# Attention steps that begin with transposes in 64-row halves and end with the values of the same unit, in a kernel of attention and two layers of experts

## The chip, the cores and the metric

The kernel runs on one core of a Trainium2 chip. The metric is the time of one execution on the device in microseconds (us). TensorE (PE) multiplies, VectorE (DVE), ScalarE (ACT) and GpSimd (POOL) work on elements, SyncE (SP) issues most DMAs. Each engine takes its own instructions in the order in which the program wrote them; between engines only semaphores hold.

## The reference, cut to what matters

```python
def _attn_ref(q, k, v):                       # (2, 8, 576, 64) each
    scores = scale * np.matmul(q, k.transpose(0, 1, 3, 2))
    mask = (rel >= 0) & (rel < 128)
    scores = np.where(mask, scores + bias[None], -1000000000.0)
    scores = scores - np.max(scores, axis=-1, keepdims=True)
    attn = np.exp(scores)
    attn = attn / (np.sum(attn, axis=-1, keepdims=True) + 1e-09)
    return np.matmul(attn, v)
...
x = attn_out.transpose(0, 2, 1, 3).reshape(1152, 512)
for e in range(4):                            # first layer
    h = np.maximum(x @ w1[e], 0.0)
    out += p[:, e:e + 1] * (h @ w2[e])
...
h = x @ w_in                                  # second layer
return (h * np.cos(h)) @ w_out
```

A query attends to itself and to 127 keys before it. All is computed in float32.

## The kernel before, in words

**Attention** (to about 78 us). Queries come in nine units of 128 rows: units 1 to 4 and 5 to 8 are rows 64 to 575 of the two batches, unit 0 holds the first 64 rows of both and comes fifth. A step is one unit and one half `g` of the eight heads; steps 0 to 17 go through `attention`. For its step `k`, `att_scores` multiplies queries by the two key blocks of the window (four matmuls on 64-row tiles into two of three banks `ps_s`; 256, 192 or, for unit 0, 64 columns), VectorE adds the bias and takes the row's minimum (four reductions, L459), and ScalarE takes four exponentials (L465) into `p`. `att_sums` adds up the denominators of a whole unit on VectorE (`rec`, L477 and L480) and GpSimd spreads them (`wide`, L482). Two steps later `att_transpose` turns `p` on TensorE (L513) and two copies, one on VectorE (L522) and one on ScalarE (L524), bring it to `pt`; `att_factors` turns `wide` (L490, copy `rs` L494). Three steps later `att_pv` multiplies by the values (L550, L539 for unit 0) and, with the second half of the heads, VectorE multiplies by the factors (L560): 128 rows of `x` are done.

**Between the groups** stands `fill(k, s)`, three places in each step. It prepares weights on GpSimd (`jobs`), from step 12 on starts matmuls of the experts (`fills`: products of the first pair of weight columns `opening`, `leftover` and `turn_rows` for the 128 rows of unit 0, and the second layer's first tile `tile_begun`, `layer2(0, 0)`), and takes up to five pieces of the transformations (`move`).

**Transformations.** The first layer multiplies 1024 of the rows by a seven-product scheme (Strassen's). Each of four column tiles of 128 needs seven operands, each in two rounded parts: `hi` is rounded on ScalarE (L342), `lo` is the rest, subtracted on VectorE or GpSimd (L177). Operands of the first batch alone come from `own` (`B11`, `B21`), the other five from `transform`: four subtractions on VectorE, five `hi`, three `lo` on VectorE and two on GpSimd. They are generators in the list `moved`, oldest first, advanced piece by piece.

**Behind the attention** `steps(0)` (L974 on) runs two pairs of weight columns against the operands (`product`, L693), sums on VectorE (L757), `finish` rounds into `hpair` (ScalarE L682, VectorE L683); then come `left` (L723), the second layer (L843), and the other eleven groups in the same way, to 648.8 us.

Of the kernel before, what the change touches and what calls it, by code (L numbers as in the profile page):

```python
# [51 lines left out]
def tile_kernel(ctx, tc, qT, kT, v, probs, w1, w2, w_in, w_out, out):  # L52
# [24 lines left out]
    ptp = ap("ptp", bufs=4)  # L77
# [271 lines left out]
    def own(t, x1):  # L349

        hi, lo = parts(t)
        if t < NP and mm is None:
            yield
            yield
        hi(B11, x1[:, 0:2])
        yield
        lo(B11, x1[:, 0:2], nc.vector)
        hi(B21, x1[:, 2:4])
        yield
        lo(B21, x1[:, 2:4], nc.gpsimd)  # L360

    def transform(t, x1, x2, ps=None):

        hi, lo = parts(t)
        t1, t2 = (txp.tile([128, 2, 128], F32, name="tx", tag="tx") for _ in range(2))
        b11, b21, b12, b22 = x1[:, 0:2], x1[:, 2:4], x2[:, 0:2], x2[:, 2:4]
        if ps is None:
            yield
            yield
            ps = x2  # L370
        else:
            nc.scalar.activation(out=x2, in_=ps, func=AF.Copy)
        sub(nc.vector, t1, ps[:, 0:2], b11)
        sub(nc.vector, t2, ps[:, 2:4], t1)
        sub(nc.vector, b12, ps[:, 2:4], b12)
        yield

        hi(T2, t2)
        yield
        lo(T2, t2, nc.gpsimd)  # L380
        hi(T1, t1)
        yield
        lo(T1, t1, nc.vector)
        hi(T3, b12)
        yield
        lo(T3, b12, nc.gpsimd)
        sub(nc.vector, b21, b21, t2)
        hi(B22, b22)
        yield
        lo(B22, b22, nc.vector)  # L390
        hi(T4, b21)
        yield
        lo(T4, b21, nc.vector)

    def transformed(*args):
        if args[0] < NP - 1 or len(args) > 3:
            move(24)
        tr = transform(*args)
        if len(args) > 3:
            next(tr)  # L400
# [11 lines left out]

    def move_together(step):

        gens = moved[::-1]
        moved.clear()
        for _ in range(3):
            next(gens[0])
        next(step, None)
        while gens:  # L420
            gens = [g for g in gens if not next(g, True)]
# [81 lines left out]
    def att_transpose(u, g, pool=ps_t, tag="t_ps"):  # L503
# [3 lines left out]
        pT = []  # L507
        for m in range(2):
            tp = pool.tile([128, 2, 2, 128], F32, name="t_ps", tag=tag)
            pt = ptp.tile([128, 2, 2, 128], F32, name="pt", tag="pt")  # L510
            for bi, (j, o, ln) in enumerate(blocks):
                for hh in range(2):
                    nc.tensor.transpose(  # L513
                        tp[:ln, bi, hh, :], p[:, 2 * m + hh, o : o + ln], ident
                    )
            if len(set(lens)) == 1:
                sl = [(slice(0, lens[0]), slice(0, len(blocks)))]
            else:
                sl = [(slice(0, lens[k]), slice(k, k + 1)) for k in range(2)]
            for a, bb in sl:  # L520
                if m == 0:
                    nc.vector.tensor_copy(pt[a, bb], tp[a, bb])  # L522
                else:
                    nc.scalar.activation(out=pt[a, bb], in_=tp[a, bb], func=AF.Copy)  # L524
            pT.append(pt)
        state[u, g] = pT

    def att_pv(u, g):
# [4 lines left out]
        for m in range(2):  # L533
            if u == 0:
                for b in range(B):
                    for hh in range(2):
# [5 lines left out]
                            pT[m][:64, 0, hh, c], start=True, stop=True,  # L542
# [4 lines left out]
            for bi, (j, o, ln) in enumerate(blocks):  # L547
                for hh in range(2):
# [4 lines left out]
                        pT[m][:ln, bi, hh, :],  # L553
                        start=(bi == 0), stop=(bi == len(blocks) - 1),
                    )
        if g == 1:
# [9 lines left out]
            else:  # L566
                t = (u - 1) % NP
                x1 = xk[:, :, t * 128 : (t + 1) * 128]
                if u <= NP:
                    normal(x1)  # L570
                    moved.append(own(t, x1))
                else:
                    normal(x2s[t % 2])
                    transformed(t, x1, x2s[t % 2])
# [11 lines left out]
    def attention(fill):  # L586
        n = len(steps)
        at = lambda k, what, *more: what(*steps[k], *more) if 0 <= k < n else None
        for k in range(n):
# [4 lines left out]
            if k < 4:  # L594
                at(k - LAG, att_transpose)
            at(k, att_scores)
            at(k - 1, att_sums)
            fill(k, 0)
            if k >= 4:
                at(k - LAG, att_transpose)  # L600
            at(k - LAG, att_factors)
            fill(k, 1)
            at(k - LAG - 1, att_pv)
            fill(k, 2)

        at(n - 1, att_sums)
        at(n - 2, att_transpose)
        fill(n, 0)
        at(n - 1, att_transpose, ps_s, "s_ps")
        at(n - 3, att_pv)  # L610
        at(n - 1, att_factors)
        fill(n, 1)
        at(n - 2, att_pv)
        fill(n, 2)
        at(n - 1, att_pv)
        fill(n + 1, 0)
# [302 lines left out]
    with tc.manual_schedule():  # L919
# [24 lines left out]
        def tile_begun():  # L944
# [5 lines left out]
            (12, 1): lambda: opening(0, 3), (13, 1): lambda: early[0],  # L950
            (14, 1): lambda: leftover(False), (15, 1): lambda: leftover(True),
            (16, 1): lambda: turn_rows(0), (17, 1): lambda: opening(1, 1),
            (18, 1): tile_begun, (19, 0): lambda: layer2(0, 0),
        }

        def fill(k, s):
            if s == 0 and k < 1:
# [4 lines left out]
            if (k, s) == (2, 0):  # L962
                for _ in range(RAWS):
                    loads_ahead()
            if (k, s) == (4, 0):
                nc.sync.dma_start(out=pr, in_=probs.rearrange("(t p) e -> p t e", p=128))
                first_bias()
            if (k, s) == (9, 0):
                routing()
            if s == 0 and 4 <= k < 18:  # L970
                for _ in range(2 if k in (13, 15) else 1):
                    next(jobs)
            step = fills.get((k, s), lambda: None)()
            if step:  # L974
                next(step)
            if (k, s) == (19, 0):
                move_together(step)
                next(early[1])
            elif (k, s) != (17, 2):
                move((0, 3, 2)[s])  # L980
            if step:
                next(step, None)

# [158 lines left out]
```

## Time and profile before

| | us |
|---|---|
| median of 3 runs | 652.18 (650.93 to 652.92) |
| profiled execution | 650.58, span 648.8 |
| TensorE busy | 637.5 (98%) |
| VectorE busy | 448.1 (69%) |
| GpSimd busy | 347.7 (54%) |
| ScalarE busy | 325.4 (50%) |
| chain that ended last | TensorE 80%, ScalarE 9%, VectorE 6% |

The granted clock of TensorE is at its upper level, 2.4 GHz, in all 40 slices. Shares are means over stages: in attention ScalarE and VectorE are far busier than over the span. A row of the timeline holds one group of equal instructions: its start, the time to the end of the last one, and in brackets what ended an idle time before it. Ends of matmuls are modelled and overlap the next group, so lengths are better read from start to start or from the chain of waits.

### The profile page before, as it was taken

To read this page: it belongs to the slowest core of one execution; us is meant where nothing else is said; L and a number is where in the kernel's file an instruction comes from. 1 tells how busy PE (TensorE), PEld (TensorE's weight loads), DVE (VectorE), ACT (ScalarE), POOL (GpSimd) and SP (SyncE) were. 2 spreads that over 40 slices of the span, in tenths; PEclk is the share of its full clock that TensorE was granted. 3 is DMA by queue.
4 is the path that set the end of the run, shared out by engine and by line. 5 is a ranking of instruction groups with operands and counts; after the bars stand their busy time and mean duration, and the time that the engine had idled before them with its cause. 6 is when DMAs were issued, how large, how long until landed. Compare 5 with 4: busy or idle time off the path is not lost.

```text
span 648.8 us, 9141 instructions
## 1 busy us (share of the span) xinstructions
PE 637.5 (98%) x3320; PEld 522.6 (81%) x3320; DVE 448.1 (69%) x778; ACT 325.4 (50%) x688; POOL 347.7 (54%) x330
## 2 busy tenths in 40 slices
PE   8999999999999999999999999999999999999988
PEld 6777778888888888888888888888778878878866
DVE  6786879879879869779689532656864654654662
ACT  6897634444454353443353421355873663763750
POOL 1677529364265175274364470583479279378340
PEclk9999999999999999999999999999999999999999
DMA  9442204425426327337153120130102202201003
GB/s 253 139 130 100 75 25 155 154 82 194 147 71 228 123 73 243 106 115 223 36 167 126 33 99 0 33 97 2 33 1 66 66 1 66 65 1 65 18 12 119
DMA packets 39421, 60.64 MB, mean 93 GB/s; under 512 B 4688, under 2 KB 21840, under 8 KB 39376
## 3 DMA queue, kind: packets, MB, share of 16 engines
q1 hardware_dynamic: 38288, 59.67, 29.0%
q8 instruction: 26, 0.43, 0.3%
q10 hardware_dynamic: 1088, 0.39, 0.2%
q14 instruction: 19, 0.16, 0.1%
HBM read 49.30 MB, written 10.75 MB: 93 GB/s over the span
## 4 chain that ended last, share of the span: by engine, by line
PE 80%; ACT 9%; DVE 6%; issue 2%; POOL 1%; DMA 1%; POOLq 0%; ACTq 0%
PE o_ps L843 41%; PE o_ps L693 29%; PE o_ps L723 4%; ACT u L646 1%; ACT p L465 1%; ACT r L647 1%; ACT u L654 1%; PE x_ps L550 1%; PE s_ps L448 1%; ACT hpair L666 1%; DVE c L757 1%; PE t_ps L513 1%; DVE p L459 1%; DMA k<-kT 1%; PE l_ps L749 1%
## 5 line engine op out<-in xcount | busy, mean ns | idle before, releaser
L843 PE MATMUL o_ps<-w2t,hpair 128*128 128x512 f32 x1140 | 269.6, 392 | 2.8 <-POOL hpair L177 2.5
L843 PEld LDWEIGHTS o_ps<-w2t,hpair 128*128 128x128 f32 x1140 | 211.0, 188 | 47.7 <-POOL hpair L177 4.7
L693 PE MATMUL o_ps<-xs,w1t 128*128 128x512 f32 x720 | 169.5, 390 | 0.4 <-DVE h L177 0.2
L693 PEld LDWEIGHTS o_ps<-xs,w1t 128*128 128x128 f32 x720 | 134.6, 188 | 29.0 <-ACT xs L342 0.5
L177 POOL TENSOR_TENSOR w1t<-raw,w1t 128x512 fp32r<-128x512 f32 x48 | 64.4, 1355 | 87.5 <-ACT w1t L200 87.1
L177 POOL TENSOR_TENSOR w2t<-raw,w2t 128x512 fp32r<-128x512 f32 x48 | 64.4, 1362 | 64.1 <-ACT w2t L200 63.8
L177 POOL TENSOR_TENSOR w1t<-sm,w1t 128x512 fp32r<-128x512 f32 x48 | 64.2, 1349 | 36.7 <-ACT w1t L200 33.3
L693 PE MATMUL o_ps<-xz,w1t 128*128 128x512 f32 x288 | 70.9, 392 | 1.7 <-DVE c L757 1.7
L177 POOL TENSOR_TENSOR hpair<-u,hpair 128x512 fp32r<-128x512 f32 x32 | 41.6, 1312 | 45.9 <-ACT hpair L666 45.9
L693 PEld LDWEIGHTS o_ps<-xz,w1t 128*128 128x128 f32 x288 | 53.5, 188 | 14.9 <-DVE c L757 2.5
L864 DVE SCALAR_TENSOR_TENSOR accpair<-o_ps,pr,accpair 128x512 f32<-128x512 f32 x56 | 41.2, 745 | 28.0 <-PE o_ps L843 28.0
L299 ACT ACTIVATE cr<-cr 128x512 f32<-128x512 f32 x32 | 21.7, 679 | 77.0 <-DVE cv L293 77.0
L683 DVE SCALAR_TENSOR_TENSOR hpair<-o_ps,hpair 128x512 fp32r<-128x512 f32 x47 | 32.4, 689 | 21.5 <-ACT hpair L682 21.5
L682 ACT ACTIVATE hpair<-o_ps 128x512 fp32r<-128x512 f32 x47 | 28.2, 599 | 36.0 <-DVE o_ps L757 36.0
L200 ACT ACTIVATE w1t<-sm 128x512 fp32r<-128x512 f32 x44 | 27.4, 624 | 29.8 <-POOL sm L177 29.8
L650 DVE SCALAR_TENSOR_TENSOR u<-r,u 128x512 f32<-128x512 f32 x36 | 30.7, 853 | 14.3 <-ACT r L647 14.3
L465 ACT ACTIVATE p<-p,nmax 128x256 f32<-128x256 f32 (+2 forms) x72 | 33.6, 468 | 13.6 <-DVE nmax L459 13.5
L723 PEld LDWEIGHTS o_ps<-w1t,x 128*128 128x128 f32 x288 | 37.7, 191 | 2.7 <-POOL w1t L177 1.0
L723 PE MATMUL o_ps<-w1t,x 128*128 128x256 f32 x288 | 39.0, 284 | 0.6 <-POOL w1t L177 0.6
L870 DVE TENSOR_TENSOR accpair<-o_ps,accpair 128x512 f32<-128x512 f32 x23 | 15.9, 690 | 32.4 <-PE o_ps L843 32.4
L289 DVE TENSOR_SCALAR cv<-cr 128x512 int32<-128x512 int32 x32 | 33.7, 1052 | 2.6 <-DMA wo<-cv 2.6
L843 PE MATMUL o_ps<-w2t,h 128*128 128x512 f32 x144 | 35.4, 392 | 0.1
(131 smaller groups left out, 872.1 us busy)
## 6 DMA issues: line engine op xcount, KB each, us to landing
raw<-w SPq DMA_DIRECT2D x32, 512.0 KB, 3.8
cr<-w_in SPq DMA_DIRECT2D x16, 512.0 KB, 4.6
cr<-w_out SPq DMA_DIRECT2D x16, 512.0 KB, 4.0
wi<-cv SPq DMA_DIRECT2D x16, 256.0 KB, 3.3
wo<-cv SPq DMA_DIRECT2D x16, 256.0 KB, 2.2
raw<-wi SPq DMA_DIRECT2D x8, 512.0 KB, 3.4
raw<-wo SPq DMA_DIRECT2D x8, 512.0 KB, 3.6
qt<-qT SPq DMA_DIRECT2D x8, 256.0 KB, 3.7
```

The source lines that it names most:

```text
L177: eng.tensor_tensor(out=out, in0=a, in1=b, op=ALU.subtract)
L200: nc.scalar.activation(out=out, in_=src, func=AF.Copy)
L289: nc.vector.tensor_scalar(out=o, in0=hw, scalar1=3, scalar2=0x3FFFFFF8, op0=ALU.logical_shift_left, op1=ALU.bitwise_and,)
L299: nc.scalar.activation(out=fl(hw), in_=fl(hw), func=AF.Abs)
L465: nc.scalar.activation(out=p[:, k, :wid], in_=p[:, k, :wid], func=AF.Exp, scale=-1.0, bias=nmax[:, k : k + 1], accum_out=den[:, k, 0:1],)
L650: nc.vector.scalar_tensor_tensor(out=u, in0=r, scalar=MAGIC, in1=u, op0=ALU.subtract, op1=ALU.subtract)
L682: nc.scalar.activation(out=hi, in_=src, func=AF.Relu)
L683: nc.vector.scalar_tensor_tensor(out=lo, in0=src, scalar=0.0, in1=hi.bitcast(F32), op0=ALU.max, op1=ALU.subtract)
L693: nc.tensor.matmul(ps, w(a, k, m), operand_of_x(bb, b)[:, m], start=(start and m == 0 and (a, bb) == PASSES[0]), stop=(stop and m == 1 and ...
L723: nc.tensor.matmul(ps[:, j * 256 : (j + 1) * 256], x0[:, bb, d, :], w_t[1, g, j][:, a, 0, d * 256 : (d + 1) * 256], start=(d == 0 and (a, ...
L843: nc.tensor.matmul(ps, hidden(a, f, t), w_t[2, g, f // 2][:, bb, f % 2, :], start=(f == 0 and (a, bb) == PASSES[0]), stop=(f == NFG - 1 an ...
L864: nc.vector.scalar_tensor_tensor(out=o, in0=ps, scalar=s, in1=o, op0=ALU.mult, op1=ALU.add)
```

## The change

Each step now begins with `att_factors` and `att_transpose` of step k - 2, then has its scores, sums, one `fill(k)` in place of three, and ends with `att_pv` of step k - 2, one step earlier than before. `att_transpose` turns each 128 by 128 block in two halves of 64 query rows: 16 matmuls with 64 columns in place of 8 with 128, the halves into different banks; VectorE copies the one half of all four heads, ScalarE the other, into one tile `pt`. `own` and `transform` of the attention become `own_early` and `transform_early`, generators with two parts, kept in `staged`; `stage`, once in each fill, advances all of them by one part. The first part of `transform_early` holds four subtractions and five `hi` (and two `lo` on GpSimd), the second three `lo` on VectorE; for the last tile (`t == NP - 1`) it pauses behind the subtractions, and fill 20 goes on with it. `layer2(0, 0)` moves from fill 19 to fill 20. No number of operations on elements changes.

```diff
-    ptp = ap("ptp", bufs=4)
+    ptp = ap("ptp", bufs=2)
...
     def own(t, x1):
 
         hi, lo = parts(t)
-        if t < NP and mm is None:
-            yield
-            yield
         hi(B11, x1[:, 0:2])
         yield
         lo(B11, x1[:, 0:2], nc.vector)
...
         yield
         lo(B21, x1[:, 2:4], nc.gpsimd)
 
-    def transform(t, x1, x2, ps=None):
+    def own_early(t, x1):
+
+        hi, lo = parts(t)
+        hi(B11, x1[:, 0:2])
+        hi(B21, x1[:, 2:4])
+        lo(B21, x1[:, 2:4], nc.gpsimd)
+        yield
+        lo(B11, x1[:, 0:2], nc.vector)
+
+    def transform_early(t, x1, x2):
 
         hi, lo = parts(t)
         t1, t2 = (txp.tile([128, 2, 128], F32, name="tx", tag="tx") for _ in range(2))
         b11, b21, b12, b22 = x1[:, 0:2], x1[:, 2:4], x2[:, 0:2], x2[:, 2:4]
-        if ps is None:
+        sub(nc.vector, t1, b12, b11)
+        sub(nc.vector, t2, b22, t1)
+        sub(nc.vector, b12, b22, b12)
+        sub(nc.vector, b21, b21, t2)
+        if t == NP - 1:
             yield
-            yield
-            ps = x2
-        else:
-            nc.scalar.activation(out=x2, in_=ps, func=AF.Copy)
+        hi(T2, t2)
+        lo(T2, t2, nc.gpsimd)
+        hi(T1, t1)
+        hi(T3, b12)
+        lo(T3, b12, nc.gpsimd)
+        hi(B22, b22)
+        hi(T4, b21)
+        yield
+        lo(T1, t1, nc.vector)
+        lo(B22, b22, nc.vector)
+        lo(T4, b21, nc.vector)
+
+    staged = []
+
+    def stage():
+
+        for st in list(staged):
+            if next(st, True):
+                staged.remove(st)
+
+    def transform(t, x1, x2, ps):
+
+        hi, lo = parts(t)
+        t1, t2 = (txp.tile([128, 2, 128], F32, name="tx", tag="tx") for _ in range(2))
+        b11, b21, b12, b22 = x1[:, 0:2], x1[:, 2:4], x2[:, 0:2], x2[:, 2:4]
+        nc.scalar.activation(out=x2, in_=ps, func=AF.Copy)
         sub(nc.vector, t1, ps[:, 0:2], b11)
...
     def transformed(*args):
-        if args[0] < NP - 1 or len(args) > 3:
-            move(24)
+        move(24)
         tr = transform(*args)
-        if len(args) > 3:
-            next(tr)
+        next(tr)
         moved.append(tr)
...
-    def move_together(step):
-
-        gens = moved[::-1]
-        moved.clear()
-        for _ in range(3):
-            next(gens[0])
-        next(step, None)
-        while gens:
-            gens = [g for g in gens if not next(g, True)]
...
-    def att_transpose(u, g, pool=ps_t, tag="t_ps"):
+    def att_transpose(u, g):
         p = state[u, g]
         blocks = list(key_blocks(place(u)[1] if u else 0))
         lens = [ln for j, o, ln in blocks]
-        pT = []
-        for m in range(2):
-            tp = pool.tile([128, 2, 2, 128], F32, name="t_ps", tag=tag)
-            pt = ptp.tile([128, 2, 2, 128], F32, name="pt", tag="pt")
-            for bi, (j, o, ln) in enumerate(blocks):
-                for hh in range(2):
-                    nc.tensor.transpose(
-                        tp[:ln, bi, hh, :], p[:, 2 * m + hh, o : o + ln], ident
-                    )
-            if len(set(lens)) == 1:
-                sl = [(slice(0, lens[0]), slice(0, len(blocks)))]
-            else:
-                sl = [(slice(0, lens[k]), slice(k, k + 1)) for k in range(2)]
-            for a, bb in sl:
-                if m == 0:
-                    nc.vector.tensor_copy(pt[a, bb], tp[a, bb])
-                else:
-                    nc.scalar.activation(out=pt[a, bb], in_=tp[a, bb], func=AF.Copy)
-            pT.append(pt)
-        state[u, g] = pT
+        tps = [ps_t.tile([128, 4, 2, 64], F32, name="t_ps", tag="t_ps") for _ in range(2)]
+        pt = ptp.tile([128, 4, 2, 128], F32, name="pt", tag="pt")
+        halves = [slice(0, 64), slice(64, 128)]
+        for bi, (j, o, ln) in enumerate(blocks):
+            for k in range(4):
+                for tp, r in zip(tps, halves):
+                    nc.tensor.transpose(tp[:ln, k, bi, :], p[r, k, o : o + ln], ident[r, r])
+        if len(set(lens)) == 1:
+            sl = [(slice(0, lens[0]), slice(0, len(blocks)))]
+        else:
+            sl = [(slice(0, lens[k]), slice(k, k + 1)) for k in range(2)]
+        for a, bb in sl:
+            nc.vector.tensor_copy(pt[a, :, bb, halves[0]], tps[0][a, :, bb, :])
+            nc.scalar.activation(out=pt[a, :, bb, halves[1]], in_=tps[1][a, :, bb, :], func=AF.Copy)
+        state[u, g] = pt
...
                 if u <= NP:
                     normal(x1)
-                    moved.append(own(t, x1))
+                    staged.append(own_early(t, x1))
                 else:
                     normal(x2s[t % 2])
-                    transformed(t, x1, x2s[t % 2])
+                    staged.append(transform_early(t, x1, x2s[t % 2]))
...
-            if k < 4:
-                at(k - LAG, att_transpose)
+            at(k - LAG, att_factors)
+            at(k - LAG, att_transpose)
             at(k, att_scores)
             at(k - 1, att_sums)
-            fill(k, 0)
-            if k >= 4:
-                at(k - LAG, att_transpose)
-            at(k - LAG, att_factors)
-            fill(k, 1)
-            at(k - LAG - 1, att_pv)
-            fill(k, 2)
-
+            fill(k)
+            at(k - LAG, att_pv)
+
+        at(n - 2, att_transpose)
         at(n - 1, att_sums)
-        at(n - 2, att_transpose)
-        fill(n, 0)
-        at(n - 1, att_transpose, ps_s, "s_ps")
-        at(n - 3, att_pv)
+        fill(n)
+        at(n - 2, att_pv)
         at(n - 1, att_factors)
-        fill(n, 1)
-        at(n - 2, att_pv)
-        fill(n, 2)
+        at(n - 1, att_transpose)
+        fill(n + 1)
         at(n - 1, att_pv)
-        fill(n + 1, 0)
+        fill(n + 2)
...
         fills = {
-            (12, 1): lambda: opening(0, 3), (13, 1): lambda: early[0],
-            (14, 1): lambda: leftover(False), (15, 1): lambda: leftover(True),
-            (16, 1): lambda: turn_rows(0), (17, 1): lambda: opening(1, 1),
-            (18, 1): tile_begun, (19, 0): lambda: layer2(0, 0),
+            12: lambda: opening(0, 3), 13: lambda: early[0],
+            14: lambda: leftover(False), 15: lambda: leftover(True),
+            16: lambda: turn_rows(0), 17: lambda: opening(1, 1),
+            18: tile_begun, 20: lambda: layer2(0, 0),
         }
 
-        def fill(k, s):
...
-            if s == 0 and 4 <= k < 18:
+            if 4 <= k < 18:
                 for _ in range(2 if k in (13, 15) else 1):
                     next(jobs)
-            step = fills.get((k, s), lambda: None)()
+            step = fills.get(k, lambda: None)()
             if step:
                 next(step)
-            if (k, s) == (19, 0):
-                move_together(step)
-                next(early[1])
-            elif (k, s) != (17, 2):
-                move((0, 3, 2)[s])
+            stage()
             if step:
                 next(step, None)
+            if k == 20:
+                next(early[1])
+                stage()
+                stage()
 
```

TensorE in steps 6 to 8 of the attention, before (`s_ps` scores, `t_ps` transposes, `r_ps` factors, `x_ps` values; `kh` is the key head of unit 0):

```order
L448 MATMUL s_ps<-k_156,qt 128x256 x4
L513 MATMUL t_ps<-ident,p 128x128 x8
L550 MATMUL x_ps<-pt,vt 64x128 x8
L448 MATMUL s_ps<-k_156,qt 128x256 x4
L513 MATMUL t_ps<-ident,p 128x128 x8
L490 MATMUL r_ps<-ident,wide 128x128 x4
L550 MATMUL x_ps<-pt,vt 64x128 x8
L442 MATMUL s_ps<-kh,qt 64x64 x8
```

And now:

```order
L533 MATMUL t_ps<-ident,p 128x64 x16
L468 MATMUL s_ps<-k_156,qt 128x256 x4
L565 MATMUL x_ps<-pt,vt 64x128 x8
L510 MATMUL r_ps<-ident,wide 128x128 x4
L533 MATMUL t_ps<-ident,p 128x64 x16
L468 MATMUL s_ps<-k_156,qt 128x256 x4
L565 MATMUL x_ps<-pt,vt 64x128 x8
L533 MATMUL t_ps<-ident,p 128x64 x16
L462 MATMUL s_ps<-kh,qt 64x64 x8
```

The factors stood behind the scores and transposes of their step; they stand ahead of both now, right behind the values of the step before.

ScalarE from the exponentials of step 17 on, before (`xs`, `xz` are the `hi` of the transformations, `rs` the copy of the factors, `x_135` and `x_136` the tiles 2 and 1, counted from 0, of the second batch):

```order
L465 ACTIVATE p,dens<-p,nmax 128x256 x4
L524 ACTIVATE pt<-t_ps 128x512
L494 ACTIVATE rs<-r_ps 128x512
L342 ACTIVATE xs<-tx 128x2x128 x2
L763 ACTIVATE p_1134<-o_ps 128x512
L524 ACTIVATE pt<-t_ps 128x512 x2
L342 ACTIVATE xs<-x_136 128x2x128
L342 ACTIVATE xz<-x_136 128x2x128
L342 ACTIVATE xz<-xk 128x2x128
L494 ACTIVATE rs<-r_ps 128x512
```

And now:

```order
L485 ACTIVATE p,dens<-p,nmax 128x256 x4
L771 ACTIVATE p_1255<-o_ps 128x512
L540 ACTIVATE pt<-t_ps 128x8x64
L342 ACTIVATE xs<-tx 128x2x128 x2
L342 ACTIVATE xs<-x_135 128x2x128
L342 ACTIVATE xz<-x_135 128x2x128
L342 ACTIVATE xz<-xk 128x2x128
L514 ACTIVATE rs<-r_ps 128x512
L540 ACTIVATE pt<-t_ps 128x8x64
```

The last two copies of `pt` stood ahead of the roundings of tile 1; now the last one stands behind all five roundings of tile 2, and tile 1 is through before.

## Rows read from the trace of the kernel before

**Rows 1.** Busy time in three stretches: PE, PEld, DVE, ACT, POOL (instructions), clock, DMA.

```profile
20.00:50.00 30.00, 29.32 (x316) 22.32 (x316) 22.07 (x103) 26.63 (x99) 23.89 (x31) 1.00 0.41 119
...
78.00:98.00 20.00, 18.48 (x84) 14.61 (x83) 15.75 (x28) 8.01 (x17) 6.37 (x8) 1.00 0.16 53
98.00:648.80 550.80, 543.82 (x2550) 451.31 (x2548) 375.13 (x521) 258.92 (x469) 295.96 (x261) 1.00 0.28 89
```

**Rows 2.** Chain of waits, TensorE's groups back to back: start, length, what.

```profile
44.61 0.61 PE x_ps L539 x16
...
49.11 1.47 PE x_ps L550 x16
...
51.65 1.02 PE t_ps L513 x8
52.67 1.43 PE o_ps L723 x12
...
57.65 0.44 PE r_ps L490 x4
...
59.52 1.02 PE x_ps L550 x16
```

**Rows 3.** Chain of waits, ScalarE in step 7: four exponentials, then a copy.

```profile
27.66 1.06 ACT p L465 x4
...
29.74 0.48 ACT pt L524
```

**Rows 4.** Timeline of TensorE: starts of scores, transposes, factors, last values.

```profile
15.27 1.14 PE L448 MATMUL s_ps<-k,qt 64*128 64x256 f32 x8
...
18.83 1.14 PE L448 MATMUL s_ps<-k,qt 64*128 64x256 f32 x8
19.89 1.10 PE L513 MATMUL t_ps<-ident,p 128*128 128x128 f32 x8
20.83 0.60 PE L490 MATMUL r_ps<-ident,wide 128*128 128x128 f32 x4
...
22.38 1.14 PE L448 MATMUL s_ps<-k,qt 64*128 64x256 f32 x8
...
45.15 1.13 PE L448 MATMUL s_ps<-kt,qt 64*128 64x256 f32 x8
...
55.49 1.14 PE L448 MATMUL s_ps<-kt,qt 64*128 64x256 f32 x8
...
64.03 1.14 PE L448 MATMUL s_ps<-kt,qt 64*128 64x256 f32 x8
...
74.84 1.97 PE L550 MATMUL x_ps<-pt,vt 128*64 128x128 f32 x32
```

**Rows 5.** Timeline: first score reduction of steps 2 and 5, factors of unit 1.

```profile
10.70 0.42 DVE L459 CUSTOM_DVE_ANT_0 p<-s_ps,bm 128x256 f32<-128x256 f32 x1 [0.23 <-PE s_ps L448]
...
13.21 0.66 PE L490 MATMUL r_ps<-ident,wide 128*128 128x128 f32 x4
...
20.00 0.42 DVE L459 CUSTOM_DVE_ANT_0 p<-s_ps,bm 128x256 f32<-128x256 f32 x1 [0.28 <-PE s_ps L448]
```

**Rows 6.** Timeline and chain of waits from step 17 to the weights at 96.67.

```profile
66.86 1.67 PE L693 MATMUL o_ps<-xs,w1t 128*128 128x512 f32 x6 [0.24 <-DVE h L177]
...
79.91 7.08 PE o_ps L693 x30
...
83.92 0.63 ACT L682 ACTIVATE hpair<-c 128x512 fp32r<-128x512 f32 x1 [0.71 <-DVE xz L177]
...
88.19 0.69 DVE c L757
...
96.67 0.75 PE o_ps L723 x4
```

**Rows 7.** Timeline of VectorE in step 15, two subtractions of tile 0.

```profile
58.65 0.42 DVE L177 TENSOR_TENSOR tx<-x,xk 128x256 f32<-128x256 f32 x1
...
59.10 1.39 DVE L177 TENSOR_TENSOR tx<-x,tx 128x256 f32<-128x256 f32 x1
```

More of the change, by code (lines that the diff above doesn't have):

```diff
@@ L541, in att_pv @@
                             v_t[b, 0][:, 64 * h : 64 * h + 64],
-                            pT[m][:64, 0, hh, c], start=True, stop=True,
+                            pT[:64, 2 * m + hh, 0, c], start=True, stop=True,
                         )
@@ L552, in att_pv @@
                         v_t[b, j][:ln, 64 * h : 64 * h + 64],
-                        pT[m][:ln, bi, hh, :],
+                        pT[:ln, 2 * m + hh, bi, :],
                         start=(bi == 0), stop=(bi == len(blocks) - 1),
@@ L949, in tile_kernel, with fill @@
         fills = {
-            (12, 1): lambda: opening(0, 3), (13, 1): lambda: early[0],
-            (14, 1): lambda: leftover(False), (15, 1): lambda: leftover(True),
-            (16, 1): lambda: turn_rows(0), (17, 1): lambda: opening(1, 1),
-            (18, 1): tile_begun, (19, 0): lambda: layer2(0, 0),
-        }
-        def fill(k, s):
-            if s == 0 and k < 1:
+            12: lambda: opening(0, 3), 13: lambda: early[0],
+            14: lambda: leftover(False), 15: lambda: leftover(True),
+            16: lambda: turn_rows(0), 17: lambda: opening(1, 1),
+            18: tile_begun, 20: lambda: layer2(0, 0),
+        }
+        def fill(k):
+            if k == 0:
                 idle = ps1.tile([128, 512], F32, name="o_ps", tag="o_ps")
@@ L961, in fill @@
                     nc.tensor.matmul(idle[:, :128], ident, ident, start=True, stop=True)
-            if (k, s) == (2, 0):
+            if k == 2:
                 for _ in range(RAWS):
                     loads_ahead()
-            if (k, s) == (4, 0):
+            if k == 4:
                 nc.sync.dma_start(out=pr, in_=probs.rearrange("(t p) e -> p t e", p=128))
                 first_bias()
-            if (k, s) == (9, 0):
+            if k == 9:
                 routing()
-            if s == 0 and 4 <= k < 18:
+            if 4 <= k < 18:
                 for _ in range(2 if k in (13, 15) else 1):
                     next(jobs)
-            step = fills.get((k, s), lambda: None)()
+            step = fills.get(k, lambda: None)()
             if step:
                 next(step)
-            if (k, s) == (19, 0):
-                move_together(step)
-                next(early[1])
-            elif (k, s) != (17, 2):
-                move((0, 3, 2)[s])
+            stage()
             if step:
                 next(step, None)
+            if k == 20:
+                next(early[1])
+                stage()
+                stage()
         attention(fill)
```

## The prediction

> **What bounds the kernel now.** I read the table by stage first. In 20 to 50 us ScalarE is busy 26.6 of 30 us and TensorE 29.3, in 78 to 98 us TensorE 18.5 of 20 [rows 1]; behind 98 us TensorE has 7 us idle in 551, and the change does not reach there [rows 1]. So I ask what each attention step waits for. I call a step's four groups on TensorE S (scores), T (transposes), P (values) and R (transposes of the factors, once per unit, which is two steps). The chain of waits gives their length back to back: T 1.02, R 0.44, P 1.02 (1.47 where a key block has 64 rows), one fill of 12 half or 6 whole matmuls about 1.4 [rows 2]; S is 1.06 (18.83 to 19.89) [rows 4]. A unit is thus 2 x (1.06 + 1.02 + 1.02) + 0.44, some 6.7 us; it takes 7.11 (15.27 to 22.38) [rows 4]. The rest goes to ScalarE, on which four exponentials take 2.08 us and a copy 0.48, all in order [rows 3].
>
> **Halved transposes.** 16 matmuls of 64 columns take the place of 8 of 128. None such is in the trace. The nearest row has 16 matmuls that move 64 columns, two at a time on different quarters of the array: 0.61 [rows 2]. The same row holds a change of tile shape, about 0.1, since T takes 1.02 before P and 0.94 before R (19.89 to 20.83), which has its shape [rows 4]. S uses 64-row tiles too, so T followed by S keeps the shape: I take 0.5. The upper end is today's 1.02 with nothing gained, the lower end half of it less the change of shape, 0.41. The gain is thus 0.5 per step on TensorE, some 9 us in 18 steps if TensorE alone set the pace. The copies to `pt` move the same number of elements; I cost them as now.
>
> The Trainium skill (TensorE: Matmul & The Clock Gate, section "LDWEIGHTS (loading the stationary operand)") says that a weight load costs columns divided by 1.2 GHz whatever the number of rows. By it 16 loads of 128 columns would need 1.7 us, or 0.85 if two row halves load side by side, and T would gain nothing. It is one of the rivals below, priced there by rows.
>
> **The new order, and its new wait.** R of a unit now opens the odd step. R needs `wide` from GpSimd, which needs `rec` from VectorE, which is queued behind the four score reductions of the even step just before. In the trace the first reduction starts 1.17 us after S begins (18.83 to 20.00), and R follows 2.51 us behind the first reduction (10.70 to 13.21) [rows 4, 5]. So R cannot start before 1.17 + 2.51 = 3.68 us after the even S. In between TensorE now has only S and P, 2.08 us: it stands for 1.6 us, with T and the next S queued behind R. Before, T and S of the next step stood in between and hid it. A unit without fill becomes, from even S to even S: 3.68, R with its change of shape 0.53, T 0.5, S 1.06, P 1.02, T 0.5 = **7.29**, against 7.11. Where a fill of 1.4 stands between S and P, the wait is covered and T's gain comes through.
>
> I walk this through, the copies on ScalarE included, and compare at the end of S (and of the fill) of step k with the start of S of step k+1 before, where the same work is done. Minus is ahead.
> - Start: the first T lets S(2) begin 0.4 earlier, at about 9.15, but VectorE gets to its reductions at 10.45 (before 10.70); R is at 10.45 + 2.51 = 12.96, then R 0.53, T 0.55, S 1.06, P 1.47, T 0.5: S(4) at 17.1, its end at 18.2 against 18.83 [rows 4]: -0.7.
> - Two units of 7.29 bring S(8) to 31.7 (the first, S(4) to S(6), took 7.11). S(8) and S(9) are 64 wide. There ScalarE holds P(6) (its copy stands behind four exponentials) until 2.6 after S(8), and P(7) until 4.55: S(10) at 37.6.
> - Unit 10, 11 (192 wide, R at 3.2): 6.15, S(12) at 43.7, with fill 46.2 against 45.15: +1.0.
> - Unit 12, 13, two fills: P ends at 3.9, behind the 3.68, so R waits for nothing; R 0.5, T 0.6, S 1.06, fill 1.4, P 1.47, T 0.5: S(14) at 53.2, with fill 55.7 against 55.49: +0.2.
> - Unit 14, 15, two fills: R at 3.68, in all 8.7: S(16) at 61.9, with the short fill of 0.53 at 63.5 against 64.03: -0.5.
>
> **Transformations in two parts.** Their instructions are the same; they now come in lumps: four subtractions on VectorE and five roundings on ScalarE (0.3 each) in one step's fill, the three other subtractions in the next. In steps 14 and 15 the copy of `pt` behind the lump is done 0.7 before P wants it, so it costs nothing. At the end it does. Step 16: R stands until 3.68 again (the fill is short), S(17) ends at 5.8. ScalarE has exponentials to 3.6, five roundings to 5.5, `h0` to 6.05; VectorE's part of `h0` (0.65) ends at 6.75, and the next fill waits for it, as in the trace it waits 0.24 for the same [rows 6]. Then fill 1.4, P(15), T(16), fill 1.5, P(16), R, T(17) until 13.35. There ScalarE first rounds tile 2 (until 13.7), then copies the factors and `pt`, until 14.7: TensorE waits 1.4, and P(17) ends at 15.8 after S(16), at 77.7 against 76.7 (74.84 and 1.9) [rows 4]: **+1.0**.
>
> Behind the attention the lumps pay. Tile 2 is already transformed, so of the last tile's work VectorE is through at 82.0 (normalization to 78.7, four subtractions to 80.3, one scaling 0.7, three subtractions 1.0). Before, `hpair` on ScalarE started at 83.92, when VectorE was through with both tiles [rows 6]. The products that TensorE starts at 79.91 start at 80.7. From 88.19 on the trace's chain is a serial one through VectorE, ScalarE and GpSimd until the weights at 96.67 [rows 6]; its first link needs five groups of six products (6.5 us) and VectorE's earlier sums. That was VectorE's before; now it is TensorE's: 80.7 + 6.5 + 0.25 = 87.45, **0.75 earlier**. What follows is paced by TensorE and moves as a whole. DMA triggers on SP keep their order; a value block is issued about 4 us before its P even so, since P comes one step earlier but each step is as long as now.
>
> **Sum.** Before's profiled execution is 650.58 (span 648.8); it lies 1.6 under the median of the three runs, 652.18. 650.58 - 0.75 = 649.8, and on the median 652.18 - 0.75 = **651.4**. Two us is about 0.3%, what a measurement here can tell from no change.
>
> **The rivals.**
> 1. VectorE stays ahead of TensorE after the last tile, and a same-shape S hides its first weight load (about 0.1 for each S in the loops of steps 4 to 11). Then the products run from 80.7 without gaps: 60 products and 12 half ones, 14.4 us in all, end at 95.1 instead of 97.4: -2.3, and with -1.1 of the loops -3.4: **648.8**. For it: TensorE has 1.5 us idle in 78 to 98 [rows 1]. Against: the serial chain until 96.67 also holds roundings of weights on ScalarE, behind `hpair` in its queue. It decides where VectorE's sums end before the products do.
> 2. Slower: the lumps are longer than priced. One subtraction of tile 0 took 1.39, the one before it 0.42, while GpSimd was busy on a tensor operation [rows 7]. If one of four takes 1 us more in each lump, `pt` or `h0` is late by 1 in steps 16 and 18 and the last tile's products by another 1, and 0.3 in step 15: 651.4 + 3.3 = **654.7**. It decides as soon as GpSimd's two subtractions of the lump before meet VectorE's four; now they are spread over three fills.
> 3. The halves gain nothing (T stays at 0.95 to 1.02). Both T of a unit lie on its loop, so 18 x 0.43 = 7.7 comes on top: **659**.
>
> **How the numbers follow.** Forecast 0.42, rival 1 0.30, rival 2 0.17, rival 3 0.11. The forecast's own range is 649.5 to 653.5: bounds are 0.5 per T less or more shared by a few loops, 0.2 per R. The range takes in rival 1 with 1.3 below it and rival 2 with 0.8 above, 647.5 to 655.5, and leaves out rival 3 and some of rival 1. Faster by over 0.3% is rival 1, 0.30; within, the forecast, 0.42; slower rivals 2 and 3, 0.28.
>
> **What would show it.** In the profile after: T followed by S in 0.45 to 0.6; TensorE idle before R, ended by GpSimd's `wide`, about 1.6 us in steps 5, 7, 11 and 17 and near none in 13; idle before the last P ended by ScalarE's `pt`, about 1.4; the first `hpair` near 82; the serial chain ending near 96. It is wrong if R comes without a wait (then it is faster by up to 1.6 per unit), if T is over 0.8, or if single subtractions of the lumps stretch.

## The result, and the profile after

| | before | after |
|---|---|---|
| median | 652.36 us (650.93 to 652.92, 4 executions) | 658.56 us (657.26 to 660.02, 4 executions) |
| ratio | | 1.0099, 95% interval 1.0072 to 1.0126 |
| profiled execution | 650.58, span 648.8 | 658.46, span 656.7 |
| mean granted clock | 1.000 | 0.994 |

The changed kernel is 1% slower, 3 us above the upper end of the range. All of it is lost in the attention, as its stage table shows beside [rows 1] (PE, PEld, DVE, ACT, POOL, clock):

```profile
20.00:50.00 30.00, 22.50 (x336) 17.62 (x333) 20.18 (x92) 23.77 (x85) 20.44 (x27) 0.94 0.43 120
78.00:98.00 20.00, 18.49 (x142) 14.68 (x141) 15.64 (x36) 8.45 (x24) 3.77 (x5) 1.00 0.23 79
98.00:656.70 558.70, 551.20 (x2586) 457.41 (x2584) 380.17 (x529) 262.47 (x475) 299.59 (x264) 1.00 0.27 88
```

TensorE, busy 29.3 of 30 us before, is busy 22.5 in 20 to 50 us, at a mean clock of 0.94. The chain of waits behind the attention answers to [rows 6]:

```profile
88.98 7.10 PE o_ps L701 x30
96.11 0.70 DVE c L765
...
104.59 0.74 PE o_ps L731 x4
```

The weights that started at 96.67 start at 104.59, 7.92 later; the span is 7.9 longer. From there on nothing is lost or won. The timeline of TensorE in steps 4 to 12 answers to [rows 4] (in brackets the wait and what ended it):

```profile
17.79 0.72 PE L533 MATMUL t_ps<-ident,p 64*128 64x64 f32 x16
18.34 1.08 PE L468 MATMUL s_ps<-k,qt 64*128 64x256 f32 x8
...
22.08 0.66 PE L510 MATMUL r_ps<-ident,wide 128*128 128x128 f32 x4 [1.42 <-POOL wide L502]
...
25.82 1.08 PE L468 MATMUL s_ps<-k,qt 64*128 64x256 f32 x8
27.59 1.09 PE L565 MATMUL x_ps<-pt,vt 128*64 128x128 f32 x16 [0.69 <-DVE pt L539]
29.94 0.66 PE L510 MATMUL r_ps<-ident,wide 128*128 128x128 f32 x4 [1.25 <-POOL wide L502]
...
33.78 0.46 PE L462 MATMUL s_ps<-kh,qt 64*64 64x64 f32 x16
36.02 1.09 PE L565 MATMUL x_ps<-pt,vt 128*64 128x128 f32 x16 [1.78 <-DVE nmax L479]
37.56 0.76 PE L510 MATMUL r_ps<-ident,wide 128*128 128x128 f32 x4 [0.45 <-POOL wide L502]
...
42.05 0.87 PE L468 MATMUL s_ps<-kt,qt 64*128 64x192 f32 x8
45.27 0.65 PE L510 MATMUL r_ps<-ident,wide 128*128 128x128 f32 x4 [1.54 <-POOL wide L502]
...
48.02 1.09 PE L468 MATMUL s_ps<-kt,qt 64*128 64x256 f32 x8
```

T takes 0.55 (17.79 to 18.34), about half of the 1.02 that it took. But every unit from step 4 to step 11 holds one wait of R for `wide`, and some hold a second, of P for the copy of its own `pt`. From 25.82 to 33.78 a unit lasts 7.96, where the unit before took 7.11 [rows 4]. Grouped over 14 to 90 us (busy and mean, then idle time before the group), before and after:

```profile
L550 PE MATMUL x_ps<-pt,vt 128*64 128x128 f32 x224 | 16.4, 281 | 0.0
L490 PE MATMUL r_ps<-ident,wide 128*128 128x128 f32 x32 | 4.9, 274 | 0.0
```

```profile
L565 PE MATMUL x_ps<-pt,vt 128*64 128x128 f32 x217 | 16.6, 287 | 5.2 <-DVE pt L539 2.0 <-DVE nmax L479 1.8 <-ACT pt L540 1.2
L510 PE MATMUL r_ps<-ident,wide 128*128 128x128 f32 x36 | 6.5, 306 | 6.3 <-POOL wide L502 6.3
```

Neither P nor R waited before; now they wait 5.2 and 6.3 us. What the halves free on TensorE (18 times 0.47, about 8.5 us by estimate) is spent standing still, and more.

What delays `pt` is VectorE's queue, which answers to [rows 5]. Two places, around step 8 and in steps 15 and 16:

```profile
33.57 1.10 DVE L177 TENSOR_TENSOR xs<-xk,xs 128x256 fp32r<-128x256 f32 x1
34.59 0.68 DVE L575 TENSOR_TENSOR xk<-x_ps,rs 128x512 f32<-128x512 f32 x1
35.20 0.67 DVE L539 COPY pt<-t_ps 128x512 f32<-128x512 f32 x1
...
66.44 1.49 DVE L177 TENSOR_TENSOR xz<-x,xz 128x256 fp32r<-128x256 f32 x1
67.86 0.82 DVE L177 TENSOR_TENSOR xz<-xk,xz 128x256 fp32r<-128x256 f32 x1
68.61 0.68 DVE L575 TENSOR_TENSOR x<-x_ps,rs 128x512 f32<-128x512 f32 x1
69.20 0.68 DVE L539 COPY pt<-t_ps 128x512 f32<-128x512 f32 x1
69.80 0.41 DVE L479 CUSTOM_DVE_ANT_0 p<-s_ps,bm 128x256 f32<-128x256 f32 x1
```

In an odd step's fill stands a `lo`, behind P the normalization, and only then come the next step's copy and its four reductions. S(16) began at 67.26; its first reduction starts 2.54 later, where step 5 before had 1.17 [rows 4, 5]. The stretched `lo` (1.49, where the shortest such takes 0.41) coincided with a subtraction on GpSimd:

```profile
66.14 1.51 POOL L177 TENSOR_TENSOR w2t<-raw,w2t 128x512 fp32r<-128x512 f32 x1
```

The end of the attention on TensorE, and its granted clock in two single microseconds (0.50, ahead of the last two numbers):

```profile
67.26 1.08 PE L468 MATMUL s_ps<-kt,qt 64*128 64x256 f32 x8
...
70.03 1.09 PE L565 MATMUL x_ps<-pt,vt 128*64 128x128 f32 x16 [1.10 <-DVE pt L539]
72.39 1.12 PE L510 MATMUL r_ps<-ident,wide 128*128 128x128 f32 x4 [1.26 <-POOL wide L502]
...
76.25 1.67 PE L701 MATMUL o_ps<-xs,w1t 128*128 128x512 f32 x6 [0.24 <-ACT rs L514]
...
84.65 1.09 PE L565 MATMUL x_ps<-pt,vt 128*64 128x128 f32 x16 [1.22 <-ACT pt L540]
```

```profile
38.00:39.00 1.00, 1.00 (x16) 0.75 (x16) 0.00 (x0) 0.69 (x2) 0.92 (x3) 0.50 0.06 16
...
73.00:74.00 1.00, 1.00 (x13) 0.67 (x13) 1.00 (x2) 0.97 (x4) 0.92 (x2) 0.50 0.41 141
```

In two stretches of the attention the clock is at its lower level, 1.2 GHz; both follow waits in close succession (1.78 and 0.45; 1.10 and 1.26). In the profiled execution before it never fell in the attention.

### The profile page after: what moved, and what is told of

Its sections match the earlier page's. It is cut to its first block, busy times and chain, and to the rows that moved or that the text cites. A ratio compares the mean times of both kernels' runs of the same rounds, so it can differ in the third digit from the quotient of the medians.

```text
span 656.7 us, 9423 instructions
## 1 busy us (share of the span) xinstructions
PE 634.8 (97%) x3456; PEld 520.5 (79%) x3456; DVE 451.1 (69%) x778; ACT 327.2 (50%) x688; POOL 347.6 (53%) x330
## 4 chain that ended last, share of the span: by engine, by line
PE 78%; DVE 9%; ACT 7%; issue 3%; POOL 1%; DMA 1%; POOLq 0%; ACTq 0%; DVEq 0%; SPq 0%
PE o_ps L851 40%; PE o_ps L701 28%; PE o_ps L731 4%; DVE p L479 3%; PE s_ps L468 1%; ACT u L654 1%; ACT r L655 1%; ACT u L662 1%; ACT hpair L674 1%; DVE c L765 1%; DVE pt L539 1%; PE t_ps L533 1%; DVE tx L177 1%; PE l_ps L757 1%; DMA k<-kT 1%
## 5 line engine op out<-in xcount | busy, mean ns | idle before, releaser
L731 PEld LDWEIGHTS o_ps<-w1t,x 128*128 128x128 f32 x288 | 37.6, 191 | 3.3 <-POOL w1t L177 0.9
```

What stands on the lines that cost most here:

```text
L731: nc.tensor.matmul(ps[:, j * 256 : (j + 1) * 256], x0[:, bb, d, :], w_t[1, g, j][:, a, 0, d * 256 : (d + 1) * 256], start=(d == 0 and (a, ...
```

## The experiments

The runs take four parts of the change apart: halves, R at the head of the step, P in the step of its own T, transformations in two parts. T at the head of the step was not undone by itself; only the first two rows have T in its old place. Each run had executions of the kernel before beside it, so the ratios compare better than the medians. "Idle" is the sum of TensorE's waits that the timeline shows between 14 and 90 us.

| kernel | R | P | transformations | median us | ratio to before (95%) | idle us |
|---|---|---|---|---|---|---|
| before (no halves) | behind fill | k - 3 | pieces | 650.7 to 652.4 | 1 | 1.8 |
| halves_before | behind fill | k - 3 | pieces | 650.63 | 0.9989 (0.9976 to 1.0002) | 5.1 |
| pv_r_late | behind fill | k - 3 | two parts | 651.35 | 0.9989 (0.9975 to 1.0002) | 7.1 |
| r_late | behind fill | **k - 2** | two parts | 657.04 | 1.0096 (1.0065 to 1.0126) | 10.6 |
| r_late_old_moves | behind fill | **k - 2** | pieces | 659.99 | 1.0128 (1.0110 to 1.0146) | 16.2 |
| pv_late | **first** | k - 3 | two parts | 658.39 | 1.0110 (1.0064 to 1.0156) | 10.9 |
| old_moves | **first** | **k - 2** | pieces | 658.61 | 1.0114 (1.0065 to 1.0164) | 11.3 |
| after | **first** | **k - 2** | two parts | 658.56 | 1.0099 (1.0072 to 1.0126) | 11.9 |

**R behind the fill again.**

```diff
-            at(k - LAG, att_factors)
             at(k - LAG, att_transpose)
...
             fill(k)
+            at(k - LAG, att_factors)
             at(k - LAG, att_pv)
```

> The changed kernel with one thing undone: R (the transposes of the factors) stands behind the fill of its step again, ahead of P, in place of opening the step. Theory A, R's new place made the loss: a wait of TensorE for `wide` with T and S queued behind it lengthens every unit of the first batch, puts S and so VectorE's reductions later, and lets the granted clock fall. Then TensorE's idle time before R is near 0 (now 1.42, 1.25, 0.45, 1.54 and 1.26 us), the clock stays at 1.00, units take 6.3 to 6.8 us from even S to even S (now 7.48 and 7.96), and the time is 649 to 653. Rival B, VectorE's queue and the lumps made the loss, R only stands where the wait would be anyhow: 656.5 to 658.5.

657.04 us: rival B's number, though not its reason. R no longer waits for `wide` (0.4 us in all), the units from S(4) to S(8) take 7.09 and 7.40, and S(16) comes at 63.40 in place of 67.26. Then the end gives back part of these 3.9 us, with spans of 654.4 and 656.7:

```profile
L565 PE MATMUL x_ps<-pt,vt 128*64 128x128 f32 x216 | 17.0, 296 | 7.4 <-DVE pt L539 3.6 <-ACT pt L540 2.0 <-DVE nmax L479 1.7
...
L510 PE MATMUL r_ps<-ident,wide 128*128 128x128 f32 x36 | 6.7, 315 | 2.8 <-DVE h L177 2.3 <-POOL wide L502 0.4
```

P now waits 7.4 us for its `pt`, and R in step 17 another 2.3 for a bank, which VectorE frees late. So theory A's time does not come: with R's wait taken away P's is 7.4 in place of 5.2. Nor did the clock stay up, as theory A had it (0.989 to 0.995 in the four executions).

**The old pieces in the new order.** `own` and `transform` as before, `move(3)` in each fill, `move(2)` behind each P, `move_together` in fill 20.

> The changed kernel with the transformations of the kernel before: pieces of one to three instructions, three in each fill and two behind each P, and the last two tiles together at the end. Theory B, the lumps made a large part of the loss (single subtractions of 1.49 where 0.41 is usual, `pt` behind `lo` B11): 653 to 655.5, with the subtractions of tiles 0 to 2 at 0.41 to 0.8 each. Rival A, R's place made it: 657 to 659, with R waiting 1.2 to 1.5 us as now.

658.61 us, so with R and P in their new places it makes no difference which form the transformations have (theory B falls). R waits 5.4 us for `wide`, as rival A said, and P another 5.5 in all.

**The halves alone.** `att_transpose` and the indices in `att_pv` as changed, all else as before.

> The kernel before with the halved transposes alone (16 of 64 columns; one copy for each half), everything else in its old place. Theory D, T stands on TensorE's path in the kernel before, which is busy 29.3 of 30 us there, and 0.5 per step comes back until ScalarE (some 6.3 us per unit) is the bound: units of 6.4 to 6.8 us in place of 7.11, time 647 to 650. Rival, the chain through reductions, exponentials and copies sets the pace and T only filled its gaps: 651.5 to 652.5.

650.63 us, between the two ranges; the ratio, 0.9989 (0.9976 to 1.0002), is not clear of no change. So most of the 8.5 us that T gives up on TensorE does not come through. T now waits 3.0 us, most of it for ScalarE's copy to free a bank:

```profile
L513 PE MATMUL t_ps<-ident,p 64*128 64x64 f32 (+1 forms) x240 | 11.9, 225 | 3.0 <-ACT pt L520 2.3 <-DVE pt L519 0.5
```

**P one step later again.**

```diff
-            at(k - LAG, att_pv)
+            at(k - LAG - 1, att_pv)
...
```

> The changed kernel with another single thing undone: P of step k - 3 ends step k, as before, so that the copies to `pt` have a step of slack again (the first part of tile 3's `own_early` is a place earlier in step 12, since the fill there reads it). Theory E, P in the step of its own T is what costs: copies on VectorE stand behind roundings' differences and a normalization, and P and all behind it wait for them. Then TensorE never waits for `pt` in steps 4 to 15, only R still waits for `wide`, about 1 us per unit, and the time is 652.5 to 655. Rival A, R's place costs as much by itself: 656 to 658.5.

658.39 us. P never waits, but R does, 1.2 to 1.8 us in each unit of the first batch:

```profile
L565 PE MATMUL x_ps<-pt,vt 128*64 128x128 f32 x224 | 17.7, 296 | 0.0
...
L510 PE MATMUL r_ps<-ident,wide 128*128 128x128 f32 x32 | 5.2, 286 | 6.1 <-POOL wide L502 6.1
```

So R's place costs as much by itself; theory E has named only one of two causes. (The lines left out move the last P behind the loop, and the first part in step 12.) Four executions took 654.46, 657.55, 659.23 and 663.38 us at mean granted clocks of 1.000, 0.995, 0.992 and 0.987: executions with a lower clock took longer. Which is cause and which effect, this scatter does not show.

**Both undone.** The two diffs together.

> The changed kernel with R behind the fill and P of step k - 3 at the end: only the halves, T at the head of the step and the transformations in two parts are left of the change. Theory E: the lumps cost nothing once the copies have slack; as the kernel before with the halves alone, 650 to 652. Rival B, the lumps cost by themselves, through subtractions stretched from 0.41 to 1.5 us while GpSimd works: 653.5 to 656.

651.35 us, ratio 0.9989, as the halves alone: on balance the lumps cost nothing once the copies have slack. P waits 0.0, R 1.5. Three waits of TensorE that the lumps' order makes are in it all the same (1.51, 1.43 and 1.70); the last version below mends them.

```profile
L565 PE MATMUL x_ps<-pt,vt 128*64 128x128 f32 x224 | 16.5, 281 | 0.0
...
L510 PE MATMUL r_ps<-ident,wide 128*128 128x128 f32 x32 | 5.0, 280 | 1.5 <-POOL wide L502 1.5
```

**P's place alone.** R behind the fill, old pieces, P in the step of its T.

> The changed kernel with R behind the fill and the transformations in small pieces as before: only the halves and P in the step of its own T are left. Theory E: P's place is the larger part of the loss, 655 to 657, with TensorE waiting for `pt` in most steps. Rival B, lumps and P's place cost only together: 651 to 653.

659.99 us, worse than expected, with P's wait the largest of all:

```profile
L545 PE MATMUL x_ps<-pt,vt 128*64 128x128 f32 x216 | 15.8, 280 | 12.9 <-DVE pt L519 8.5 <-DVE nmax L459 2.6 <-DVE rec L477 1.8
```

The two executions at a clock of 0.999 took 659.40 each, so nearly all of this is waiting. With pieces in place of lumps the median is 3 us above that of r_late, though the two intervals overlap; why pieces are worse here was not tested.

**The clock.** Matmuls of the identity where TensorE waits.

```diff
+        ps = ps1.tile([128, 512], F32, name="o_ps", tag="o_ps")
+        for _ in range(n):
+            nc.tensor.matmul(ps[:, :128], ident, ident, start=True, stop=True)
...
```

> The changed kernel with matmuls of the identity by itself (3 to 12 of 128 columns, no result used) in the places where TensorE waits: ahead of R in steps 5, 7, 9, 11 and 17 and ahead of P in step 8. The waits stay, only TensorE is busy in them. Theory C, the two stretches at the lower clock level (0.50, about 38 to 41.3 and 72.4 to 75.8 us) cost what T, S and R take longer there, 1.5 to 3 us: 655.5 to 657, clock 1.00 behind the first 10 us. Rival, the slower matmuls lie in time that TensorE would wait anyhow, or the added ones stand in the way: 658 to 659.5.

662.39 us, and useless as a test: ten of them take 2.50 us (each counts as two records), longer than the waits.

```profile
21.30 2.50 PE L507 MATMUL o_ps<-ident 128*128 128x128 f32 x20
```

> As keep_clock, with fewer matmuls, since one of 128 columns turned out to take 0.23 us and the added ones outlasted the waits: 5, 4, 5 and 4 of them ahead of R in steps 5, 7, 11 and 17, and 5 ahead of P in step 8, each sum shorter than the wait that it stands in (1.42, 1.25, 1.54, 1.26 and 1.78 us). Theory C, the lower clock level is a loss of its own on top of the waits: in the executions of pv_late 654.46, 657.55, 659.23 and 663.38 us go with mean granted clocks of 1.000, 0.995, 0.992 and 0.987, 8.9 us for 0.013 of the clock, and the changed kernel's profiled execution (0.994) should lose 0.006 of 656.7, 3.9 us, to it. Then the time is 654 to 656 with a clock of 0.997 or more. Rival, work at the lower clock only fills waits: 658 to 659.5.

658.96 us. Two of its four executions held a clock of 1.000 (657.06 and 657.72 us), two did not (660.20 at 0.994, 662.87 at 0.989), so the median tests little. In the profiled execution (span 655.2) the clock stayed at 1.00, and this one execution can be compared with the profiled one after step by step:

```profile
20.00:50.00 30.00, 26.91 (x376) 21.17 (x374) 20.72 (x97) 24.48 (x89) 21.74 (x27) 1.00 0.44 125
```

```profile
32.85 0.46 PE L462 MATMUL s_ps<-kh,qt 64*64 64x64 f32 x16
...
40.09 0.87 PE L468 MATMUL s_ps<-kt,qt 64*128 64x192 f32 x8
...
70.80 0.66 PE L518 MATMUL r_ps<-ident,wide 128*128 128x128 f32 x4 [0.18 <-POOL wide L502]
...
74.66 1.66 PE L711 MATMUL o_ps<-xs,w1t 128*128 128x512 f32 x6 [1.65 <-ACT rs L522]
```

From S(8) to S(10) it took 7.24 (32.85 to 40.09) and 8.27 in the changed kernel (33.78 to 42.05): the first stretch of low clock cost 1.0. In step 17 the fill starts 3.86 behind R in both (70.80 to 74.66, and 72.39 to 76.25), waiting for the copy `rs` behind ScalarE's roundings: there the low clock only filled that wait. So in these two executions theory C's 3.9 us is 1.0, and the rival is mostly right; for the other executions no trace shows where the clock fell.

**What keeps the halves from paying.** In halves_before VectorE stands idle for ScalarE's rounding, with the next reductions behind it:

```profile
22.86 1.13 DVE L177 TENSOR_TENSOR xs<-xk,xs 128x256 fp32r<-128x256 f32 x1 [1.77 <-ACT xs L342]
```

```diff
         hi(B11, x1[:, 0:2])
+        if t < NP and mm is None:
+            hi(B21, x1[:, 2:4])
+            lo(B21, x1[:, 2:4], nc.gpsimd)
+            for _ in range(5 if t < NP - 1 else 3):
+                yield
+            lo(B11, x1[:, 0:2], nc.vector)
+            return
```

> The kernel before with the halves, and one thing more: in the first batch `lo` of B11 on VectorE comes after the next step's reductions instead of ahead of them, where VectorE now stands idle 1.77 us for ScalarE's rounding with the reductions queued behind it. Theory F, that queue is what keeps the units at 7 us when T is halved: units of 6.3 to 6.6 us in steps 6 to 11, TensorE ahead by 1.5 to 3 us at step 12, time 647.5 to 649.5. Rival, ScalarE's own work sets the unit: 650 to 651.

649.64 us, ratio 0.9972 (0.9958 to 0.9985), 0.14 above theory F's range; its interval overlaps that of halves_before. The unit from S(6) to S(8) takes 6.52 (21.52 to 28.04) in place of 7.86, as theory F said, but at S(12) TensorE is only 1.2 ahead of halves_before (39.31 against 40.48). The edit also brings the rounding of B21 and its `lo` on GpSimd forward. So theory F holds for this unit; what it gains in time over halves_before is not clear of noise.

**A version that beats both.** pv_r_late already has that `lo` behind the reductions. Three places at which its TensorE still waited were mended:

```diff
+            if k == 12:
+                stage()
             at(k, att_scores)
...
-            stage()
+            if k == 15:
+                next(step, None)
+            if k == 20:
+                next(staged[-1])
+            elif k != 12:
+                stage()
```

> pv_r_late (halves, T at the head of the step, transformations in two parts; R and P as before) with three places mended at which its trace still shows TensorE waiting: 1.51 us in step 12 for `lo` B11 of the last tile (now ahead of the scores), 1.43 in step 16 for `lt` behind five roundings (now ahead of them) and 1.70 for the last tile's roundings, whose subtractions stand behind three `lo` of the tile before (now ahead of them). Theory E, with slack for the copies TensorE is the bound and gets these back: 647 to 649. Rival, VectorE and ScalarE are the bound by then and the waits come up elsewhere: 650.5 to 652.

`best` had at k == 20 all of the newest tile's and the older tile's pieces, newest first, ahead of `acc`. 650.56 us: two of the waits went and one shrank to 0.68, but a new one of 2.85 stood behind them. `best_2` has the lines above.

> As best, but in the last fill only the last tile's four subtractions come first, then the sum `acc` of the second layer's first tile, then the three `lo` of the tile before. In best TensorE was 2 us ahead of pv_r_late at 74.7 us and lost 2.85 there, waiting for that sum to free a bank. Theory E: the wait goes, the thirty products start near 77.5 us in place of 79.1, and the time is 648 to 649.5. Rival, another wait of the same size stands behind it: 650 to 651.

646.75 us (646.39 to 648.42), ratio 0.9936 (0.9922 to 0.9950): better than expected. The thirty products of `best`, then those of `best_2` and its weights, which start at 92.68 where [rows 6] had 96.67:

```profile
79.10 8.70 PE L704 MATMUL o_ps<-xs,w1t 128*128 128x512 f32 x30 [2.85 <-DVE acc L873]
```

```profile
77.09 7.06 PE L704 MATMUL o_ps<-xs,w1t 128*128 128x512 f32 x30 [0.80 <-ACT xz L342]
...
92.68 0.74 PE L734 MATMUL o_ps<-w1t,x 128*128 128x256 f32 x4 [0.26 <-POOL w1t L177]
```

In `best` they took 8.70, with the clock at its lower level there in that execution (mean 0.54 in 80 to 82 us). So the halves, T at the head of the step and the two parts, with the three places mended, are worth 4 us when R and P stay where they were; without the mending they were worth nothing that can be told from noise.

**A fall of the clock that the change has no part in.** Near the end every profiled kernel has the same wait of 1.33 us. In the profiled executions of pv_r_late (mean 0.55 in 630 to 632 us), halves_before, halves_lo_late and `best` the clock fell behind it; in those of the kernel before, best_2 and all the others it stayed up. The 58 matmuls there take 1.65 longer at the lower level; pv_r_late, then before:

```profile
627.63 15.09 PE L852 MATMUL o_ps<-w2t,hpair 128*128 128x512 f32 x58 [1.33 <-POOL hpair L177]
```

```profile
629.23 13.44 PE L843 MATMUL o_ps<-w2t,hpair 128*128 128x512 f32 x58 [1.32 <-POOL hpair L177]
```

So differences of 1 to 2 us between single executions say nothing of the attention.

## Why the prediction was wrong

Its forecast was 651.4, its range 647.5 to 655.5; 658.56 came. Its marks against the trace:

| mark | forecast | measured | added here |
|---|---|---|---|
| S(4) | 17.1 | 18.34 | 1.2 |
| S(8) | 31.7 | 33.78 | 0.8 |
| S(10) | 37.6 | 42.05 | 2.4 |
| S(16) | 61.9 | 67.26 | 0.9 |
| P(17) ends | 77.7 | 85.7 | 2.6 |
| first sum of the serial chain | 87.45 | 96.11 | 0.7 |

The sum, 8.6, is the 7.9 that came and the 0.75 that was forecast to be gained.

- **Halves: right.** T took 0.55 for a forecast 0.5, so rival 3 is out; that its 659 lies next to the 658.56 that came is chance. There was luck in the 0.5 too: the row of 0.61 that it was read from holds 8 matmuls with two records each, not 16 matmuls. The weight-load rule of the Trainium skill (TensorE: Matmul & The Clock Gate, section "LDWEIGHTS (loading the stationary operand)") ties a weight load to its columns, whatever the number of rows; by an estimate from it T would have stayed at 0.85 or more. The trace, with 0.55, does not agree.
- **P in the step of its own T: the step that failed.** The change's part on it was not priced at all in units of 256 columns. The walk let P follow S, with the copy to `pt` done by then. It was not: P(4) waited 0.69 and P(14) 1.10, where the walk has no wait. VectorE's `lo` and normalization stand ahead of the copy and of the even step's reductions. The row that the walk used, a first reduction 1.17 behind S, was from an odd step; the even steps 6, 8 and 16 had 1.55, 2.01 and 2.54. r_late against pv_r_late: P's place alone takes 5.7 us (657.04 - 651.35). Putting P back does not bring the forecast time, though (pv_late, 658.39): a second term failed with it.
- **R's wait: right in size; the gain it was set against did not come.** R came 3.74, 4.12, 3.78 and 3.22 behind the even S in steps 5, 7, 9 and 11 (forecast 3.68, and 3.2 for 192 columns), and waited 1.25 to 1.54 in steps 5, 7 and 11. In step 17 it came 5.13 behind S(16), since the reductions were late. pv_late against pv_r_late shows that R's place alone takes 7.0 us (658.39 - 651.35). Even at a clock of 1.000 it is 5.6 (654.46 against 648.87, one execution each). The walk set this against T's gain and came out near even, but halves_before shows T's gain alone to be about nothing in time (0.9989). From S(12) to S(16), where the walk has two fills in each unit and T's gain coming through, it had 18.2; the changed kernel took 19.24 (48.02 to 67.26), the kernel before 19.75:

```profile
40.73 1.14 PE L448 MATMUL s_ps<-kt,qt 64*128 64x256 f32 x8
...
60.48 1.13 PE L448 MATMUL s_ps<-kt,qt 64*128 64x256 f32 x8
```

- **The two do not add.** By the medians either alone costs 5.7 to 7.0 and both together 7.2 (658.56 - 651.35); by the ratios it is 7.0 for P, 7.9 for R and 7.2 for both, so they can't be ranked. That is why undoing one part at a time showed almost nothing. The waits of P and R together are 10.2 us with P's place alone, 6.1 with R's alone, 11.5 with both and 1.5 with neither. Why they overlap, in that both hold up the same loop, is argued from this and not shown by a run.
- **S(8) to S(10), 2.4 too long.** 1.0 is the lower clock, which the prediction had not foreseen. In the rest stand the waits of R(9) and P(7), 0.45 and 0.48 in keep_clock_2 at full clock.
- **The end: half right.** The last P waited 1.22 for ScalarE's `pt` (forecast 1.4). But fill 17 came 8.99 behind S(16), not 6.99; 1.4 of these 2.0 is VectorE, which reached S(16)'s reductions 2.54 behind S, not 1.17.
- **Rival 2, stretched lumps: seen, and not the cause.** Single subtractions took 1.49 and 1.50 while GpSimd subtracted, which the prediction named as a sign of being wrong. But on balance the lumps cost nothing in pv_r_late, and with R and P early it made no difference to have pieces in their place (old_moves).
- **Behind the attention the lumps pay: partly right.** From the end of P(17) to the first sum of the serial chain 10.4 us passed, 11.5 before [rows 4, 6], 9.75 by the forecast.
- **0.9 of the 1.2 at S(4)** is most likely that execution's own start: keep_clock_2, the same up to there, had S(4) at 17.43.

## What to carry to other kernels

An engine that is 98% busy in a stage need not be the bound of a loop whose instructions are in a fixed order: here TensorE was 98% busy, and half of T's time taken away brought 0.1%. Price a reordering by the slack between producer and consumer on every queue in between, and take each duration from a row of the same place in the loop (even or odd step). When undoing one part of a change shows nothing, undo pairs: of two waits in one loop each can cost the whole loss by itself, and parts that cost nothing can be kept. A wait that is mended must be followed to the next one in line, as `best` and `best_2` show.

## What was not expected of the hardware

TensorE's granted clock fell to its lower level after waits of 1 to 2 us, in a stage where it was full in the profiled execution before, and what that costs depends on the place: 1.0 us in steps 8 to 10, nothing in step 17, 1.65 in the 58 matmuls near the end. The same wait does not always bring it down: behind the 1.33 near the end it fell in some profiled executions and not in others. In best_2, five executions at clocks of 0.999 to 1.000 took 646.39 to 646.88, the sixth, at 0.997, 648.42. The kernels with more stalls also scatter more: 654.46 to 663.38 for pv_late. The stretched subtractions on VectorE (0.41 at the shortest, up to 1.50 while GpSimd subtracts) were known from [rows 7], at 1.39; that they coincide with GpSimd's was read from rows, and no run took GpSimd's work away to show the cause.
